# A two-stage kernel on one core: rows of results stored in order, and five pieces of weights put together by TensorE

## The chip, the cores and the metric

The kernel runs on one core of a Trainium2 chip. A core has five engines with a queue of instructions each: TensorE (PE; the loading of its weights, PEld, is listed apart), VectorE (DVE), ScalarE (ACT), GpSimd (POOL) and SyncE (SP), which here issues nearly all transfers. Transfers run on 16 DMA engines. Data lie in HBM, in SBUF (128 partitions) and, for the results of matmuls, in PSUM. The metric is the time of one execution on the device in microseconds (us).

## The reference

Attention without a softmax, with a norm over each head, and then a softplus layer between two matrix products. Cut to what is computed:

```python
# q, k, v: (8, 8, 576, 64), float32; g_norm: (64,)
kv  = np.einsum('bhsd,bhse->bhde', k, v)
o   = np.einsum('bhsd,bhde->bhse', q, kv)
rms = np.sqrt(np.mean(o * o, axis=-1, keepdims=True) + 1e-06)
x   = (o / rms * g_norm)          # -> (4608, 512) after transpose and reshape
# w_in: (512, 2048), w_out: (2048, 512); both arrive as float64
h   = x @ w_in
g   = np.maximum(h, 0.0) + np.log1p(np.exp(-np.abs(h)))
out = (g @ w_out).astype(np.float32)      # (4608, 512)
```

The two large products are made exact enough with float32r matmuls: each operand is split into a high part, a low part scaled by 4096 and a combination of the two, and three matmuls are summed. The weights are 8-byte words, of which the kernel takes the two halves apart and puts float32 numbers together.

## The kernel before

The kernel does not issue instructions directly. It adds tasks to a plan (engine, estimated duration, what it comes after, a priority `pos`, buffers it takes and gives back). `Plan.order` then simulates the engines and gives the order in which every task is issued. So a change of any priority or duration can reorder all five queues. TensorE's idle time before the first big matmul is filled by the plan with matmuls that compute nothing (`warm`).

The sequence of 4608 rows is cut into 36 tiles of 128 rows and 12 blocks of three tiles. The feed-forward part runs in 192 steps: a step takes one block of rows and one of 16 pieces of the inner dimension. The steps are grouped in three phases with partial sums kept in HBM between them.

Constants that the change replaces: the priorities of the first eight pieces of weights (`CONVERT`, and `FETCH` for their loads), of the early tiles, and of the later pieces.

```python
P0 = [-93.0, -6.2, -50.8, -8.7, -11.6, -1.5, -14.9, 2.7, -53.5, -34.8, ...]
CONVERT, FETCH, EARLY, LATER = P0[:8], P0[8:16], P0[16:27], P0[27:]
BY_PE = 12                     # tiles from here on are turned by VectorE
```

One piece of weights (128 x 512) becomes float32 in `weight`. It is cut here to what each instruction does; the line of the profile stands beside it:

```python
a1 = ACT square      # L286: sq <- raw
d1 = DVE high1       # L290: t <- bits of the upper word
d2 = DVE high2       # L294: t <- sign and exponent bits
d3 = DVE mask        # L299: t <- (sq is large enough) * t
     ACT beyond      # L303: sum that shows values out of range
d4 = DVE power       # L307: p <- exponent of t
d5 = DVE rest        # L312: p <- lower word * 2**-52 * p
     DVE total       # L316: w <- t + p
```

Then `divide` splits w in three. For the first four pieces of each matrix (`by_pe`) the last difference is taken by TensorE:

```python
def high():     # ACT, L348
    nc.scalar.activation(dst.tile[:, 0], w.tile, func=AF.Copy, scale=DOWN)
def low():      # DVE, L351: d <- w - high
    nc.vector.tensor_tensor(out=d, in0=w.tile, in1=dst.tile[:, 0], op=ALU.subtract)
def low_up():   # ACT, L355
    nc.scalar.activation(dst.tile[:, 1], d.tile, func=AF.Copy, scale=RADIX)
def less_by_pe():   # PE, L366 and L367
    nc.tensor.matmul(y, lhsT=ident_r, rhs=dst.tile[:, 0], start=True, stop=False)
    nc.tensor.matmul(y, lhsT=minus_r, rhs=dst.tile[:, 1], start=False, stop=True)
def third_of_bank():   # ACT, L370
    nc.scalar.activation(dst.tile[:, 2], bank.tile, func=AF.Copy, scale=-E / (1.0 + E))
```

The attention part of a tile of rows: q is turned (L578 and L585, or by VectorE from the third batch on), multiplied by kv (L523; kv itself is L506), squared (ACT, L591), summed (DVE, L528), its root taken (POOL, L531 and L532), and normed (DVE, L535). The first 12 tiles are turned by TensorE (L540) and stored; of these, the first blocks are also split at once (ACT L437, DVE L440 and L444). Later tiles are turned by VectorE in blocks of 32 x 32 (L615), and the three tiles of a block are put side by side and stored together:

```python
n, i = divmod(t, TB)                      # TB = 3
...   # turn_blocks: xb.tile[:, :, i] <- 32 x 32 blocks of x, turned
def store(a):      # L619
    nc.sync.dma_start(out=xd[n][:, a * TB * BL:(a + 1) * TB * BL].rearrange("(b i) m -> i b m", i=BL),
                      in_=xb.tile[a * BL:(a + 1) * BL].rearrange("i b t j -> i b (t j)"))
...
if i == TB - 1:    # four stores when the third tile is turned
```

So the columns of such a block in HBM are not in the order of the rows of the sequence: groups of 32 rows of the three tiles alternate.

A step, and what ends a block:

```python
def mm1():       # L658, 12 matmuls: h <- x (384 rows) by one piece of w_in
def mm2(i):      # L665, 3 matmuls for each of three tiles: s_i <- g by w_out
# between them: softplus (ACT L678), high (ACT L680), low and less (DVE L669, L673)

def leave(ph, t, bank, done, pos):
    ...          # DVE, L705: ot <- bank * scale + partial sum (loaded by L703)
    if ph == LAST and t >= BY_PE:
        n, i = divmod(t, TB)
        def store():
            m = 0
            while m < P // BL:
                a, u = divmod(P // BL * i + m, TB)
                k = min(TB - u, P // BL - m)
                nc.sync.dma_start(        # L716
                    out=out[n * NT:(n + 1) * NT].rearrange("(t s) f -> t s f", t=TB)[u:u + k, a * BL:(a + 1) * BL],
                    in_=ot.tile[m * BL:(m + k) * BL])
                m += k
        ...
        return
    ...          # all others: nc.sync.dma_start(out=dst, in_=ot.tile), L724, 128 x 512 at once
```

For the blocks whose rows alternate, L716 puts groups of 32 rows back in their places: a tile of results leaves as a piece of 3x32 rows and one of 32, or as two of 2x32 rows.

Of the kernel before, what the change touches and what calls it, by code (L numbers as in the profile page):

```python
# [8 lines left out]
F32 = mybir.dt.float32  # L9
F32R = mybir.dt.float32r  # L10
U32 = mybir.dt.uint32
BF16 = mybir.dt.bfloat16
AF = mybir.ActivationFunctionType
ALU = mybir.AluOpType
# [4 lines left out]
P = 128  # L19
EPS = 1e-6  # L20
RADIX = 4096.0
# [19 lines left out]
class Plan:  # L41
# [13 lines left out]
    def slot(self, ring):  # L55
        return Slot(ring)
# [86 lines left out]
def kernel(  # L143
# [31 lines left out]
    NT = 384  # L175
# [7 lines left out]
    PLACES = 8  # L183
    LAST = PHASES[-1]

    P0 = [-93.0, -6.2, -50.8, -8.7, -11.6, -1.5, -14.9, 2.7, -53.5, -34.8, -51.7, -14.7, -24.2, 1.3,
          -0.2, -4.2, 2.5, -13.0, 8.5, 9.5, 5.5, 23.5, -2.0, 2.5, 2.5, 7.0, 5.0, 14.5, 9.0, 44.5, 49.5,
          68.5, 52.5, 72.0, 95.5, 100.5, 114.5, 111.0, 116.5, 8.5]
    CONVERT, FETCH, EARLY, LATER = P0[:8], P0[8:16], P0[16:27], P0[27:]
    BY_PE = 12  # L190
    AT_ONCE = 2 * TB

# [66 lines left out]
    def weight(j, pos, fetch_pos):  # L259

        c, of_out = divmod(j, 2)
        raw, w = slot("raw"), slot("m")
        words = 2 if wide else 1  # L270

        def fetch():
            src = w_source(j)
            x = new(raw, [P, d_model, words], U32 if wide else F32)
            nc.sync.dma_start(
                out=x.rearrange("p n w -> p (n w)").rearrange("p (a f) -> p a f", a=src.shape[1]), in_=src)

        f = add("SP", 450, fetch, (), fetch_pos, [raw], size=1800, behind=int(pos) - 3)
        if wide:
            sq, t, p = (slot(n) for n in ("sq", "m", "m"))  # L280

            def words_of():
                return raw.tile[:, :, 0], raw.tile[:, :, 1]

            def square():
                nc.scalar.activation(new(sq, [P, d_model], BF16), raw.tile.bitcast(BF16)[:, :, 3],  # L286
                                     func=AF.Square, scale=2.0 ** 47)

            def high1():
                nc.vector.tensor_scalar(out=new(t, [P, d_model], U32), in0=words_of()[1], scalar1=3,  # L290
                                        scalar2=0x3FFFFFF8, op0=ALU.logical_shift_left, op1=ALU.bitwise_and)

            def high2():
                nc.vector.scalar_tensor_tensor(out=t.tile, in0=words_of()[1], scalar=0xC0000000, in1=t.tile,  # L294
                                               op0=ALU.bitwise_and, op1=ALU.bitwise_or)

            def mask():
                tf = t.tile.bitcast(F32)
                nc.vector.scalar_tensor_tensor(out=tf, in0=sq.tile, scalar=2.0 ** 64, in1=tf,  # L299
                                               op0=ALU.is_ge, op1=ALU.mult)  # L300

            def beyond():
                nc.scalar.activation(sq.tile, sq.tile, func=AF.Identity, scale=2.0 ** -126, bias=big,  # L303
                                     accum_out=over[:, j:j + 1])

            def power():
                nc.vector.tensor_scalar(out=new(p, [P, d_model], U32), in0=t.tile, scalar1=0xFF800000,  # L307
                                        scalar2=None, op0=ALU.bitwise_and)

            def rest():  # L310
                pf = p.tile.bitcast(F32)
                nc.vector.scalar_tensor_tensor(out=pf, in0=words_of()[0], scalar=2.0 ** -52, in1=pf,  # L312
                                               op0=ALU.mult, op1=ALU.mult)

            def total():
                nc.vector.tensor_tensor(out=new(w, [P, d_model]), in0=t.tile.bitcast(F32),  # L316
                                        in1=p.tile.bitcast(F32), op=ALU.add)

            a1 = add("ACT", 670, square, [f], pos, [sq], [raw])
            d1 = add("DVE", 430, high1, [f], pos, [t], [raw])  # L320
            d2 = add("DVE", 690, high2, [d1], pos, [], [raw])
            d3 = add("DVE", 690, mask, [d2, a1], pos, [])
            over_done.append(add("ACT", 910, beyond, [d3], pos + (4 if c < 4 else 0), [], [sq]))
            d4 = add("DVE", 430, power, [d3], pos, [p, w])
            d5 = add("DVE", 690, rest, [d4], pos, [], [raw])
            ready = add("DVE", 690, total, [d3, d5], pos, [], [t, p])
        else:
            ready = add("DVE", 450, lambda: nc.vector.tensor_copy(new(w, [P, d_model]), raw.tile[:, :, 0]),
                        [f], pos, [w], [raw])
        if c < PLACES or first_step[c] - last_step[c - PLACES] > 12:  # L330
            divide(j, w, ready, pos, "m", c < 4)
        else:
            spilled = dram.tile([P, d_model], F32, name=f"w_spill{j}")
            st = add("SP", 350, lambda: nc.sync.dma_start(out=spilled, in_=w.tile), [ready], pos, [], [w], 900)
            again = slot("x" if of_out else "m")
            back = max(last_step[c - PLACES] + 0.5, first_step[c] - 3)
            ld = add("SP", 350, lambda: nc.sync.dma_start(out=new(again, [P, d_model]), in_=spilled),
                     [st], back, [again], [], 900, behind=last_step[c - PLACES] - 1)
            divide(j, again, ld, back, "m")

    def divide(j, w, ready, pos, ring, by_pe=False):

# [173 lines left out]
    def rows(t):  # L516
# [88 lines left out]


        n, i = divmod(t, TB)
        if i == 0:
            xb_slots[n] = slot("xb"), []
        xb, turns = xb_slots[n]  # L610

        def turn_blocks():
            if i == 0:
                new(xb, [P, d_model // BL, TB, BL])
            nc.vector.transpose(out=xb.tile[:, :, i], in_=x.tile.rearrange("p h d -> p (h d)").rearrange(  # L615
                "p (b j) -> p b j", j=BL))

        def store(a):
            nc.sync.dma_start(out=xd[n][:, a * TB * BL:(a + 1) * TB * BL].rearrange("(b i) m -> i b m", i=BL),  # L619
                              in_=xb.tile[a * BL:(a + 1) * BL].rearrange("i b t j -> i b (t j)"))  # L620

        turns.append(add("DVE", 710, turn_blocks, [a], pos, [] if i else [xb], [x], follows=turns[-1] if i else None))
        if i == TB - 1:
            stores = [add("SP", 450, lambda a=a: store(a), turns, pos + 0.5, [], [xb], 820) for a in range(P // BL)]
            for u in range(n * TB, t + 1):
                x_there[u] = stores

    def x_of(t):
# [66 lines left out]
    def leave(ph, t, bank, done, pos):  # L695

        ot = slot("m" if ph == 0 else ("m", "x", "m")[t % TB] if ph == LAST else "m")
        if ph == 0:
            a = add("ACT", 600, lambda: nc.scalar.activation(new(ot, [P, d_model]), bank.tile, func=AF.Copy, scale=1.0 + E),
                    [done], pos, [ot], [bank])  # L700
        else:
            pt = slot("m")
            ld = add("SP", 350, lambda: nc.sync.dma_start(out=new(pt, [P, d_model]), in_=part[ph - 1, t][0]),  # L703
                     [part[ph - 1, t][1]], pos - EARLY[10], [pt], [], 900, behind=int(pos) - 4)
            a = add("DVE", 700, lambda: nc.vector.scalar_tensor_tensor(  # L705
                out=new(ot, [P, d_model]), in0=bank.tile, scalar=(scale if ph == LAST else 1.0 + E), in1=pt.tile,
                op0=ALU.mult, op1=ALU.add), [done, ld] + (scale_done if ph == LAST else []), pos, [ot], [bank, pt])
        if ph == LAST and t >= BY_PE:
            n, i = divmod(t, TB)

            def store():
                m = 0
                while m < P // BL:
                    a, u = divmod(P // BL * i + m, TB)
                    k = min(TB - u, P // BL - m)
                    nc.sync.dma_start(  # L716
                        out=out[n * NT:(n + 1) * NT].rearrange("(t s) f -> t s f", t=TB)[u:u + k, a * BL:(a + 1) * BL],
                        in_=ot.tile[m * BL:(m + k) * BL])
                    m += k

            part[ph, t] = None, add("SP", 800, store, [a], pos, [], [ot], 750)
            return
        dst = out[t * P:(t + 1) * P] if ph == LAST else dram.tile([P, d_model], F32, name=f"part{ph}_{t}")
        st = add("SP", 350, lambda: nc.sync.dma_start(out=dst, in_=ot.tile), [a], pos, [], [ot], 720)  # L724
        part[ph, t] = dst, st
# [88 lines left out]
```

## Time and profile before

| | |
|---|---|
| time, median of 3 runs | 934.63 us (933.73 to 934.82) |
| span of the profiled execution | 932.7 us (its time: 934.44 us) |
| mean granted TensorE clock | 0.989 |
| busy PE / PEld / DVE / ACT / POOL | 97% / 88% / 67% / 44% / 9% of the span |
| moved by DMA | 131.43 MB, 141 GB/s in the mean |

The page gives shares of the whole span; the kernel has a head (attention of the first tiles, the first weights), a long middle, and a tail (the last results on their way out). A wait is read in the stretch in which it stands: the timeline shows instructions in order of time, with the idle time before them in brackets; the chain of waits goes back from the last instruction to what released it. In a line of the timeline the first two numbers are start and duration in us. In a line of a group, the number after the bar is the busy time in us, then the mean duration in ns, then the idle time of the engine before them. Matmuls are pipelined, so the distance from one start to the next says more than a duration.

### The profile page before, as it was taken

The page shows a single profiled execution, that of the slowest core. Times are in us where ns is not written, and L with a number is a line of the kernel's source. Part 1 is how long each engine was busy: PE and PEld are TensorE (multiplying, and loading weights), DVE is VectorE, ACT ScalarE, POOL GpSimd, SP SyncE. Part 2 cuts the span into 40 slices and gives each one's busy share as a digit, 9 for nine tenths or more (in the row PEclk, how much of TensorE's full clock was granted, in tenths as well). Part 3 has the DMA queues.
Part 4 walks back from the last instruction along what each step waited for, and adds up shares of the span by engine and source line. Part 5 has one row for each costly group of instructions (what it writes and reads, how often), then busy time and mean ns, then how long its engine had stood idle before and what let it go on. Part 6 is the DMA issues. An engine that isn't in the chain of part 4 may idle for free.

```text
span 932.7 us, 13257 instructions
## 1 busy us (share of the span) xinstructions
PE 904.9 (97%) x4821; PEld 818.5 (88%) x4821; DVE 627.3 (67%) x1055; ACT 414.5 (44%) x799; POOL 80.4 (9%) x78
## 2 busy tenths in 40 slices
PE   7899999999999999999999999999999999999992
PEld 5689899989999999999999999989999998999992
DVE  6777788776458887788757878887434455655531
ACT  4766555444433656464424455555322323333320
POOL 0323421221113100000000000000000000000000
PEclk8999999999999999999999999999999999999997
DMA  8999998498782554346334445551231233444321
GB/s 213 225 225 222 248 212 205 102 212 151 171 143 90 147 147 136 112 145 206 102 102 128 148 157 169 189 182 39 85 102 56 81 102 102 106 119 127 109 75 42
DMA packets 231377, 131.43 MB, mean 141 GB/s; under 512 B 130448, under 2 KB 205200, under 8 KB 231312
## 3 DMA queue, kind: packets, MB, share of 16 engines
q1 hardware_dynamic: 231152, 130.58, 53.3%
q8 instruction: 38, 0.62, 0.3%
q14 instruction: 27, 0.22, 0.1%
q10 hardware_dynamic: 160, 0.00, 0.0%
HBM read 91.75 MB, written 38.80 MB: 140 GB/s over the span
## 4 chain that ended last, share of the span: by engine, by line
PE 93%; SPq 2%; DVE 1%; DMA 1%; POOL 1%; ACT 1%; issue 0%; ACTq 0%
PE s L665 43%; PE h L658 43%; PE o L523 3%; PE o L506 3%; SPq L568 1%; DMA g_col<-in_g_norm_dram 1%; PE tp L540 0%; POOL r L532 0%; DMA m<-in_v_dram 0%; DMA qa<-in_q_dram 0%; DVE m L312 0%; PE tp L578 0%; DVE r L528 0%; DVE xv L440 0%; DVE m L316 0%
## 5 line engine op out<-in xcount | busy, mean ns | idle before, releaser
L658 PE MATMUL h<-xv,w 128*128 128x384 f32 x2304 | 434.6, 337 | 0.0
L665 PE MATMUL s<-w,gv 128*128 128x512 f32 x1728 | 434.3, 395 | 0.0
L658 PEld LDWEIGHTS h<-xv,w 128*128 128x128 f32 x2304 | 406.2, 188 | 14.8 <-issue 0.2
L665 PEld LDWEIGHTS s<-w,gv 128*128 128x128 f32 x1728 | 319.5, 188 | 59.1 <-issue 0.5
L678 ACT ACTIVATE g<-h 128x384 f32<-128x384 f32 x192 | 94.3, 491 | 398.4 <-PE h L658 394.4
L669 DVE TENSOR_TENSOR gv<-g,gv 128x384 fp32r<-128x384 f32 x192 | 106.6, 555 | 175.9 <-ACT gv L680 175.0
L680 ACT ACTIVATE gv<-g 128x384 fp32r<-128x384 f32 x192 | 100.9, 525 | 23.3 <-PE s L665 16.6
L673 DVE SCALAR_TENSOR_TENSOR gv<-gv 128x384 fp32r<-128x384 f32 x192 | 107.0, 557 | 6.0
L440 DVE SCALAR_TENSOR_TENSOR xv<-m,g_col,xv 128x512 fp32r<-128x512 f32 x102 | 75.8, 743 | 1.1 <-ACT xv L437 1.1
L444 DVE SCALAR_TENSOR_TENSOR xv<-xv 128x512 fp32r<-128x512 f32 x108 | 74.5, 690 | 2.6
L437 ACT ACTIVATE xv<-m,g_down 128x512 fp32r<-128x512 f32 x102 | 69.7, 710 | 2.5 <-DMA m<-x 2.4
L532 POOL TENSOR_TENSOR r<-r,half 128x8 f32<-128x8 f32 x36 | 65.8, 1826 | 3.0
L506 PEld LDWEIGHTS o<-m,m 128*128 128x128 f32 x256 | 34.2, 200 | 8.7 <-issue 7.3
L506 PE MATMUL o<-m,m 128*128 128x128 f32 x256 | 35.4, 285 | 6.4 <-DMA m<-in_v_dram 6.4
L705 DVE SCALAR_TENSOR_TENSOR m<-s,scale,m 128x512 f32<-128x512 f32 x24 | 17.9, 747 | 29.7 <-PE s L665 29.7
L523 PE MATMUL o<-kv_diag,m 128*128 128x128 f32 (+1 forms) x296 | 36.9, 275 | 0.0
L523 PEld LDWEIGHTS o<-kv_diag,m 128*128 128x128 f32 (+1 forms) x296 | 35.0, 179 | 1.8 <-issue 1.0
L531 POOL TENSOR_SCALAR r<-r 128x8 f32<-128x8 f32 x36 | 13.9, 386 | 244.9 <-DVE r L528 244.8
L535 DVE TENSOR_TENSOR x<-o,r 128x512 f32<-128x512 f32 x33 | 22.7, 688 | 17.6 <-POOL r L532 17.6
L528 DVE TENSOR_REDUCE r<-x 128x8 f32<-128x512 f32 x36 | 24.5, 681 | 13.3 <-ACT x L591 13.2
L705 DVE SCALAR_TENSOR_TENSOR m<-s,m 128x512 f32<-128x512 f32 x36 | 23.3, 684 | 10.2 <-PE s L665 10.1
L286 ACT ACTIVATE sq<-raw 128x512 bf16<-128x512 bf16 x32 | 21.3, 665 | 16.4 <-DMA raw<-in_moe_w_in_dram 10.2
(67 smaller groups left out, 445.6 us busy)
## 6 DMA issues: line engine op xcount, KB each, us to landing
m<-x SPq DMA_DIRECT2D x102, 256.0 KB
part<-m SPq DMA_DIRECT2D x72, 256.0 KB
m<-part SPq DMA_DIRECT2D x72, 256.0 KB
raw<-in_moe_w_in_dram SPq DMA_DIRECT2D x16, 512.0 KB
m<-in_k_dram SPq DMA_DIRECT2D x64, 128.0 KB
m<-in_v_dram SPq DMA_DIRECT2D x32, 256.0 KB
raw<-in_moe_w_out_dram SPq DMA_DIRECT2D x16, 512.0 KB
qa<-in_q_dram SPq DMA_DIRECT2D x24, 288.0 KB
```

Of the source, the lines that this page charges most:

```text
L437: nc.scalar.activation(cols(0, F32R), x.tile, func=AF.Identity, scale=g_down)
L440: nc.vector.scalar_tensor_tensor(out=cols(1, F32R), in0=x.tile, scalar=g_col, in1=cols(0), op0=ALU.mult, op1=ALU.subtract)
L444: nc.vector.scalar_tensor_tensor(out=cols(2, F32R), in0=cols(1), scalar=-RADIX, in1=cols(0), op0=ALU.mult, op1=ALU.add)
L506: nc.tensor.matmul(kv[:, i if tail else p], lhsT=l, rhs=r, start=(p == 0 and i == 0), stop=tail, skip_group_check=True)
L523: nc.tensor.matmul(y[r0:r0 + n, p::NP], lhsT=qT.tile[:, p, r0:r0 + n], rhs=kv_diag[b % 2][:, p].rearrange("r (h d) -> r h d", d=D), start= ...
L532: nc.gpsimd.tensor_tensor(out=r.tile, in0=r.tile, in1=half, op=ALU.pow)
L658: nc.tensor.matmul(hp, lhsT=w_in.tile[:, i, kd * P:(kd + 1) * P], rhs=xv.tile[:, i, kd], start=(m == 0), stop=(m == 3 * KD - 1))
L665: nc.tensor.matmul(mine[i].tile, lhsT=gv.tile[:, m, i * P:(i + 1) * P], rhs=w_out.tile[:, m], start=(c == cs[0] and m == 0), stop=(c == cs ...
L669: nc.vector.tensor_tensor(out=gv.tile[:, 1], in0=g.tile, in1=gv.tile.bitcast(F32)[:, 0], op=ALU.subtract)
L673: nc.vector.scalar_tensor_tensor(out=gv.tile[:, 2], in0=f32[:, 1], scalar=-RADIX, in1=f32[:, 0], op0=ALU.mult, op1=ALU.add)
L678: a = add("ACT", 490, lambda: nc.scalar.activation(new(g, [P, NT]), h.tile, func=AF.Softplus, scale=1.0 + E), [a], s, [g], [h])
L680: a = add("ACT", 530, lambda: nc.scalar.activation(new(gv, [P, 3, NT], F32R)[:, 0], g.tile, func=AF.Copy, scale=DOWN), [a], s, [gv])
```

## The change

It has three parts.

The results: the last block of rows is turned and stored tile by tile in the order of its rows (`g = 1`), so that its results leave by the plain store of 128 x 512. The results of the other alternating blocks leave in pieces of 32 rows, each a store of its own, where a piece could hold 2x32 or 3x32 rows before. This is meant to spread each store over all DMA engines.

The weights: for the five pieces with the earliest priority, VectorE no longer adds the two halves and no longer takes the low part; TensorE sums both halves less the high part in PSUM with three matmuls, one of them in float32. ScalarE takes the high part of the upper half alone. This is meant to relieve VectorE at the start.

The priorities: all of `P0` may differ, and with it the order of the queues.

```diff
-    P0 = [-93.0, -6.2, -50.8, -8.7, -11.6, -1.5, -14.9, 2.7, -53.5, -34.8, -51.7, -14.7, -24.2, 1.3,
-          -0.2, -4.2, 2.5, -13.0, 8.5, 9.5, 5.5, 23.5, -2.0, 2.5, 2.5, 7.0, 5.0, 14.5, 9.0, 44.5, 49.5,
-          68.5, 52.5, 72.0, 95.5, 100.5, 114.5, 111.0, 116.5, 8.5]
+    P0 = [-98.5, -5.2, -28.3, -7.2, -15.1, -5.0, -33.4, 1.2, -54.5, -41.8, -53.2, -12.2, -29.2, 0.3,
+          -0.7, -5.2, 1.0, -14.5, 9.0, 9.5, 5.5, 24.5, -2.0, 2.5, 2.5, 2.5, -14.5, 14.5, 9.0, 44.5,
+          49.5, 68.5, 52.5, 73.0, 96.0, 100.0, 114.5, 111.0, 116.0, 8.5]
+    BY_TENSOR = sorted(range(8), key=lambda j: CONVERT[j])[:5]
...  # in weight():
+            def rest_rounded():
+                nc.vector.scalar_tensor_tensor(out=new(w, [P, d_model], F32R), in0=words_of()[0], scalar=2.0 ** -52,
+                                               in1=p.tile.bitcast(F32), op0=ALU.mult, op1=ALU.mult)
+            if j in BY_TENSOR:
+                d4 = add("DVE", 430, power, [d3], pos, [p, w])
+                d5 = add("DVE", 690, rest_rounded, [d4], pos, [], [raw, p])
+                divide_by_pe(j, t, w, d3, d5, pos)
+                return
...  # new:
+    def divide_by_pe(j, t, p, t_there, p_there, pos):
+        def high():
+            nc.scalar.activation(new(dst, [P, 3, d_model], F32R)[:, 0], t.tile.bitcast(F32), func=AF.Copy, scale=DOWN)
+        def low():
+            y = new(banks[0], [P, d_model])
+            nc.tensor.matmul(y, lhsT=ident, rhs=t.tile.bitcast(F32), start=True, stop=False)
+            nc.tensor.matmul(y, lhsT=ident_r, rhs=p.tile, start=False, stop=False)
+            nc.tensor.matmul(y, lhsT=minus_r, rhs=dst.tile[:, 0], start=False, stop=True)
+        def low_up():
+            nc.scalar.activation(dst.tile[:, 1], banks[0].tile, func=AF.Copy, scale=RADIX)
...  # less (two matmuls) and third as before, from banks[1]
...  # x of the later tiles:
         n, i = divmod(t, TB)
+        g = TB if n < n_blocks - 1 else 1
+        i0, i = i - i % g, i % g
...
-                new(xb, [P, d_model // BL, TB, BL])
+                new(xb, [P, d_model // BL, g, BL])
...
-            nc.sync.dma_start(out=xd[n][:, a * TB * BL:(a + 1) * TB * BL].rearrange("(b i) m -> i b m", i=BL),
+            nc.sync.dma_start(out=xd[n][:, i0 * P + a * g * BL:i0 * P + (a + 1) * g * BL].rearrange("(b i) m -> i b m", i=BL),
...  # in leave():
-        if ph == LAST and t >= BY_PE:
+        if ph == LAST and BY_PE <= t < n_tiles - TB:
...
-                m = 0
-                while m < P // BL:
+                for m in range(P // BL):
                     a, u = divmod(P // BL * i + m, TB)
-                    k = min(TB - u, P // BL - m)
-                    nc.sync.dma_start(
-                        out=out[n * NT:(n + 1) * NT].rearrange("(t s) f -> t s f", t=TB)[u:u + k, a * BL:(a + 1) * BL],
-                        in_=ot.tile[m * BL:(m + k) * BL])
-                    m += k
+                    row = n * NT + u * P + a * BL
+                    nc.sync.dma_start(out=out[row:row + BL], in_=ot.tile[m * BL:(m + 1) * BL])
```

More of the change, by code (lines that the diff above doesn't have):

```diff
@@ L339, in weight, with less, third @@
             divide(j, again, ld, back, "m")
+    def divide_by_pe(j, t, p, t_there, p_there, pos):
+        c, of_out = divmod(j, 2)
+        dst = slot(f"w{of_out}_{c % PLACES}")
+        w_slots[of_out, c] = dst
+        banks = [slot("h"), slot("h")]
+        def high():
[7 more added lines that the diff above has]
+            nc.scalar.activation(dst.tile[:, 1], banks[0].tile, func=AF.Copy, scale=RADIX)
+        def less():
+            y = new(banks[1], [P, d_model])
+            nc.tensor.matmul(y, lhsT=ident_r, rhs=dst.tile[:, 0], start=True, stop=False)
+            nc.tensor.matmul(y, lhsT=minus_r, rhs=dst.tile[:, 1], start=False, stop=True)
+        def third():
+            nc.scalar.activation(dst.tile[:, 2], banks[1].tile, func=AF.Copy, scale=-E / (1.0 + E))
+        a = add("ACT", 640, high, [t_there], pos, [dst])
+        b = add("PE", 1500, low, [a, p_there], pos, [banks[0]], [t, p])
+        e = add("ACT", 600, low_up, [b], pos, [], [banks[0]])
+        b2 = add("PE", 500, less, [e], pos, [banks[1]])
+        e2 = add("ACT", 600, third, [b2], pos, [], [banks[1]])
+        factors_done[of_out, c] = [a, e, e2]
     def divide(j, w, ready, pos, ring, by_pe=False):
@@ L618, in store @@
         def store(a):
-            nc.sync.dma_start(out=xd[n][:, a * TB * BL:(a + 1) * TB * BL].rearrange("(b i) m -> i b m", i=BL),
+            nc.sync.dma_start(out=xd[n][:, i0 * P + a * g * BL:i0 * P + (a + 1) * g * BL].rearrange("(b i) m -> i b m", i=BL),
                               in_=xb.tile[a * BL:(a + 1) * BL].rearrange("i b t j -> i b (t j)"))
         turns.append(add("DVE", 710, turn_blocks, [a], pos, [] if i else [xb], [x], follows=turns[-1] if i else None))
-        if i == TB - 1:
-            stores = [add("SP", 450, lambda a=a: store(a), turns, pos + 0.5, [], [xb], 820) for a in range(P // BL)]
-            for u in range(n * TB, t + 1):
+        if i == g - 1:
+            stores = [add("SP", 450, lambda a=a: store(a), turns, pos + 0.5, [], [xb], 820 if g > 1 else 490)
+                      for a in range(P // BL)]
+            for u in range(t - i, t + 1):
                 x_there[u] = stores
@@ L707, in leave @@
                 op0=ALU.mult, op1=ALU.add), [done, ld] + (scale_done if ph == LAST else []), pos, [ot], [bank, pt])
-        if ph == LAST and t >= BY_PE:
+        if ph == LAST and BY_PE <= t < n_tiles - TB:
             n, i = divmod(t, TB)
             def store():
-                m = 0
-                while m < P // BL:
+                for m in range(P // BL):
                     a, u = divmod(P // BL * i + m, TB)
-                    k = min(TB - u, P // BL - m)
-                    nc.sync.dma_start(
-                        out=out[n * NT:(n + 1) * NT].rearrange("(t s) f -> t s f", t=TB)[u:u + k, a * BL:(a + 1) * BL],
-                        in_=ot.tile[m * BL:(m + k) * BL])
-                    m += k
-            part[ph, t] = None, add("SP", 800, store, [a], pos, [], [ot], 750)
+                    row = n * NT + u * P + a * BL
+                    nc.sync.dma_start(out=out[row:row + BL], in_=ot.tile[m * BL:(m + 1) * BL])
+            part[ph, t] = None, add("SP", 1600, store, [a], pos, [], [ot], 750)
             return
```

## The prediction

> **What bounds the kernel now.** I read the chain of waits first.
>
> ```profile
> PE 93%; SPq 2%; DVE 1%; DMA 1%; POOL 1%; ACT 1%; issue 0%; ACTq 0%
> ```
>
> TensorE holds 93% of the chain. Its two big groups, and the slices:
>
> ```profile
> L658 PE MATMUL h<-xv,w 128*128 128x384 f32 x2304 | 434.6, 337 | 0.0
> L665 PE MATMUL s<-w,gv 128*128 128x512 f32 x1728 | 434.3, 395 | 0.0
> ...
> PE   7899999999999999999999999999999999999992
> ```
>
> Neither group has idle time before it. In the chain in order of time, twelve L658 take 2.10 us and nine L665 about 2.08 us, so one of the 192 steps costs 4.18 us and all cost 802 us. From 60 us to 916 us the TensorE row has no gap. Only two places can give time: the head, before that unbroken stretch, and the tail after it. The timeline of the tail:
>
> ```profile
> 911.89 4.37 PE L665 MATMUL s<-w,gv 128*128 128x512 f32 x18
> ...
> 916.30 0.75 DVE L705 SCALAR_TENSOR_TENSOR m<-s,scale,m 128x512 f32<-128x512 f32 x1
> ...
> 918.64 1.29 SPq L716 DMA_DIRECT2D out_dram<-m  x2
> ```
>
> The last arithmetic ends at 917.05, the last store is issued by 919.9, the span ends at 932.7: 15.6 us of nothing but stores. The waits of the SyncE queue say what for:
>
> ```profile
> SPq L809 <- DMA out_dram<-m: 11.6, 1, 11.6
> ```
>
> Two stretches show how fast stores go (busy us of PE, PEld, DVE, ACT, POOL, then clock, DMA share, GB/s). At 651 the queue stores whole tiles by L724; at 921 it drains L716's stores:
>
> ```profile
> 651.00:653.00 2.00, 2.00 (x13) 1.91 (x12) 1.32 (x2) 0.35 (x1) 0.00 (x0) 1.00 0.50 183
> 921.00:931.00 10.00, 0.00 (x0) 0.00 (x0) 0.00 (x0) 0.00 (x0) 0.00 (x0) 0.50 0.16 51
> ```
>
> A share of 0.16 is 2.6 engines of 16, and 51 GB/s over them is 20 GB/s each. The drain is not short of bandwidth, it is spread over too few engines.
>
> The head, TensorE first:
>
> ```profile
> 40.20 1.13 PE L506 MATMUL o<-m,m 128*128 128x128 f32 x8 [1.68 <-DMA m<-in_v_dram]
> ...
> 43.35 0.60 PE L540 MATMUL tp<-ident_r,x 128*128 128x128 f32 x4
> ...
> 46.38 2.35 PE L658 MATMUL h<-xv,w 128*128 128x384 f32 x12
> ...
> 54.75 1.13 PE L506 MATMUL o<-m,m 128*128 128x128 f32 x8 [1.34 <-DMA m<-in_v_dram]
> ```
>
> The first step starts at 46.38, after the third tile's turn at 43.35, and that one stands behind a group that waits for v. VectorE meanwhile mixes weights (L316, L351) with rows of x (L535, L440):
>
> ```profile
> 26.20 0.69 DVE L316 TENSOR_TENSOR m<-m,m 128x512 f32<-128x512 f32 x1
> 26.82 0.69 DVE L351 TENSOR_TENSOR m<-m,w 128x512 f32<-128x512 f32 x1
> ...
> 31.32 0.69 DVE L535 TENSOR_TENSOR x<-s,r 128x512 f32<-128x512 f32 x1 [0.76 <-POOL r L532]
> ...
> 40.38 0.68 DVE L535 TENSOR_TENSOR x<-s,r 128x512 f32<-128x512 f32 x1
> ...
> 45.18 0.75 DVE L440 SCALAR_TENSOR_TENSOR xv<-tp,g_col,xv 128x512 fp32r<-128x512 f32 x1 [1.92 <-ACT m L600]
> ```
>
> Start to start, L316 and L351 cost 0.6 us each. VectorE is full from 10.7 to 38 us; after that it waits for the chain through GpSimd, TensorE and ScalarE.
>
> **What the Trainium skill says.** "DMA: Bandwidth & Descriptors", section "Why a DMA increments its semaphore by 16 and not by 1": a copy runs on the largest k up to 16 that divides the slowest dimension above 1 of both patterns, and uses the lowest-numbered engines. L716's pieces of 3x32 rows (from 96 partitions) then get 3 engines, those of 2x32 get 2, and a plain 32-row piece gets 16. The 2.6 engines above agree. The section on the anatomy of one DMA in the same page says that most of the fixed cost is the write receipt; here the span goes on for about 1.2 us after data stop (no GB in the stretch 932 to 933, 6 GB/s in the one before). "FP8 and Floating Point Precision", "TensorE Precision Notes": true fp32 takes four passes. Here four fp32 matmuls of 128 columns (L506) take 0.89 us and one fp32r matmul of 512 columns (L366, L367) 0.23 us: a ratio of nearly four for as many columns.
>
> **Part 1: the stores at the end.** Before, each of the last three tiles is 256 KB. By the rule, engine 0 gets 64 KB of the first tile's 192 KB piece, 64+64 KB of the second tile's two pieces, 64 KB of the third's, and 2x4 KB of the plain pieces: 264 KB, at 20 GB/s 13.5 us. From about 917 that ends near 930.5; the trace has data until 931-932. After, the last block is stored in the order of its rows, so its tiles go by the whole-tile store: 16 KB per engine and tile. The third is ready at 917.05; its issue takes 0.34 us (the duration of L724's), then an estimated 0.6 us to the first byte (L724's at 649.97 had data in the stretch from 650), 16 KB at 20 GB/s take 0.8 us, the receipt 1.2 us: 920.0. If the three tiles instead share the 183 GB/s that L724 showed, 786 KB take 4.3 us from 916.4, and the end is 921.9. I take 921.0: 11.7 us off the tail, all of it on the path. This is the part I trust most.
>
> **Part 2: weights by TensorE.** Each of five pieces loses L316 and L351, 1.2 us of VectorE, 6 us in all, none on ScalarE. TensorE gets three more matmuls a piece: one fp32 of 512 columns (0.89) and two fp32r (0.24 each), 1.4 us, in all 6.8 us. In the order of the changed kernel four of the five come before the first step; there stand 28 warm-up matmuls of L778 where 44 stood, so 16 x 0.24 = 3.8 us of the added 5.5 us take the place of work that does nothing, the rest that of idle time. The order of loads up to q's is the same, and the first x tile waits for them, so 31.3 us for its norm should hold. Then VectorE has less in between: I follow the third tile, its norm at 39.3 instead of 40.4. Its turn still stands behind the group that waits for v at 40.2, but without the group for the tail: near 41.9 instead of 43.35. ScalarE and VectorE follow, and the first step starts near 44.8: 1.6 us earlier, not 6. After it, the fifth piece adds 1.4 us to a full TensorE; the third step now stands ahead of the group that waited 1.34 us at 54.75, which hides that wait; and a piece of weights (512 KB, 2.2 us at the 240 GB/s or so of 50 to 100 us) is now fetched ahead of two of batch 2's keys and values, which may cost 0 to 2 us. Sum: -1.6 + 1.4 - 1.3 + 1.0 = -0.5 us.
>
> **Part 3: the middle.** Blocks 4 to 10 store each tile in four pieces instead of two; four issues of 0.34 us cost the queue what two of 0.7 cost. The last block's x goes out in 12 stores with runs of 128 bytes instead of 4 with 384; the DMA share there is 0.3 to 0.5 and x is read much later. The new constants put loads of partial sums behind the stores of the block before, with 20 us (five steps) to spare. None of it lies on the path: 0.
>
> **Sum.** Span 932.7 - 11.7 - 0.5 = 920.5; the time is 1.8 us above the span now, so 922.3 us, 1.3% less.
>
> **Rivals.** First, VectorE binds the head: it is full from 10.7 to 38 us, and six microseconds less work would bring the first step 5 to 6 us forward, to a time near 917. Against it: the waits for v at 40.2 and for GpSimd stay. Second, TensorE's added work is not hidden: the granted clock is 0.5 in the stretches from 8 to 14 us, the first piece's fp32 matmul falls there and takes twice as long, and kv's groups stand behind it; with loads shifted too, the head loses 3 to 5 us and the time is near 927. Third, stores spread over all engines were hidden anyway and the tail is the receipt of the writes: then nothing changes but the head, and the time stays at 934. The 11.6 us wait with data moving at 51 GB/s speaks against that.
>
> **Range and chances.** The tail is uncertain by 1 us, the head by 3 us either way, and new constants can open a wait in the middle: 919.5 to 927. Faster by over 2% needs 915.9, that is 6 us more from the head: 0.04. Slower by over 2% would take a new stall of 30 us: 0.01. Within 2%: 0.95.
>
> **What would show it.** Right: the SyncE queue's last wait for out_dram falls from 11.6 us to about 2 to 3; the last stretch runs at over 150 GB/s; the span goes on 3 to 5 us after the last VectorE instruction instead of 15.6; the first L658-like group starts at 44 to 46 us; steps stay at 4.18 us. Wrong: gaps in TensorE between 60 us and the end, a first step later than 47 us, or last data still over 10 us after the last arithmetic.

## The result, and the profile after

| | before | after |
|---|---|---|
| time, median | 934.66 us (933.73 to 934.82) | 922.35 us (922.26 to 922.57) |
| span of the profiled execution | 932.7 us | 920.6 us |
| first step starts | 46.38 us | 45.03 us |
| last arithmetic ends | 917.05 us | 917.44 us |
| span goes on after it | 15.6 us | 3.2 us |

The ratio is 0.987, with a 95% interval of 0.985 to 0.989. The chain by engine and the last wait of the SyncE queue, after:

```profile
PE 95%; DMA 2%; SPq 1%; ACT 1%; DVE 1%; issue 0%; ACTq 0%; DVEq 0%
```

```profile
SPq L852 <- DMA out_dram<-m: 1.7, 1, 1.7
```

TensorE's share of the chain is larger because the span lost what was not TensorE: the wait of 11.6 us for the last results is 1.7 us now. The timeline of the tail after, and then two stretches of it (busy us of PE, PEld, DVE, ACT and POOL, clock, DMA share, GB/s):

```profile
912.27 4.38 PE L712 MATMUL s<-w,gv 128*128 128x512 f32 x18
...
916.69 0.75 DVE L752 SCALAR_TENSOR_TENSOR m<-s,scale,m 128x512 f32<-128x512 f32 x1
916.77 0.34 SPq L767 DMA_DIRECT2D out_dram<-x  x1
917.47 0.33 SPq L767 DMA_DIRECT2D out_dram<-m  x1
```

```profile
917.00:919.00 2.00, 0.00 (x0) 0.00 (x0) 0.44 (x1) 0.00 (x0) 0.00 (x0) 1.00 0.99 371
...
919.00:920.00 1.00, 0.00 (x0) 0.00 (x0) 0.00 (x0) 0.00 (x0) 0.00 (x0) 1.00 0.04 12
```

The share is 0.99: all 16 engines move data, at 371 GB/s together and 23 GB/s each. The three tiles (786 KB) are out by 919.1, where 51 GB/s needed until 931 before. The last multiplication and the last addition come no earlier than before. So the whole gain is in the tail, and the head gave nothing. The experiments test both halves of that sentence.

### The profile page after: what moved, and what is told of

Its sections match the earlier page's. It is cut to its first block, busy times and chain, and to the rows that moved or that the text cites. A ratio compares the mean times of both kernels' runs of the same rounds, so it can differ in the third digit from the quotient of the medians.

```text
span 920.6 us, 13308 instructions
## 1 busy us (share of the span) xinstructions
PE 907.2 (99%) x4824; PEld 818.8 (89%) x4824; DVE 620.2 (67%) x1045; ACT 414.6 (45%) x799; POOL 78.7 (9%) x78
## 4 chain that ended last, share of the span: by engine, by line
PE 95%; DMA 2%; SPq 1%; ACT 1%; DVE 1%; issue 0%; ACTq 0%; DVEq 0%
PE s L712 43%; PE h L705 43%; PE o L567 3%; PE o L550 3%; DMA g_col<-in_g_norm_dram 1%; DMA raw<-in_moe_w_in_dram 1%; PE tp L584 1%; SPq L612 0%; DMA qa<-in_q_dram 0%; PE tp L622 0%; PE s L567 0%; SPq L534 0%; PE h L363 0%; ACT sq L304 0%; DVE xv L484 0%
## 5 line engine op out<-in xcount | busy, mean ns | idle before, releaser
L550 PEld LDWEIGHTS o<-m,m 128*128 128x128 f32 x256 | 33.6, 197 | 2.2 <-issue 0.7
L550 PE MATMUL o<-m,m 128*128 128x128 f32 x256 | 34.8, 281 | 0.1
L300 DVE SCALAR_TENSOR_TENSOR m<-sq,m 128x512 f32<-128x512 bf16 x32 | 22.0, 689 | 10.8 <-ACT sq L287 9.5
```

The source lines that it names most:

```text
L550: nc.tensor.matmul(kv[:, i if tail else p], lhsT=l, rhs=r, start=(p == 0 and i == 0), stop=tail, skip_group_check=True)
```

## The experiments

Two theories stood against each other for the tail. Mine: a store is cut over as many DMA engines as the shape of its pieces allows, and the old shapes gave 2 or 3 engines, always the same ones. The rivals: the gain comes from the head, or the old tail was a matter of one queue, or of scattered rows. For the head, mine was that loads and the chain of the first tiles bind it, so that VectorE's saved work and TensorE's added work about cancel; the rival was that VectorE binds it.

### The last block alone

The kernel before, with the last block of rows in order, and nothing else of the change:

```diff
 # kernel before
+        g = TB if n < n_blocks - 1 else 1
+        i0, i = i - i % g, i % g
...
-        if ph == LAST and t >= BY_PE:
+        if ph == LAST and BY_PE <= t < n_tiles - TB:
```

> The kernel before, with only the last block of rows turned and stored in the order of its rows, so that its three tiles of results leave by the whole-tile store; weights, priorities and all other stores are as before. Theory (the gain is the tail alone, because the last stores run on 2 or 3 engines): 922 to 923.5 us, the last data about 2 us after the last arithmetic, the span 3 to 4 us after it. Rival (the head, with weights by TensorE and new priorities, gives a part): above 925 us. Rival (the tail is the receipt of the writes): 934 us.

Measured: 921.36 us, ratio 0.987 (0.985 to 0.988). The last arithmetic ends at 917.69, the span at 920.7, 3.0 us later. One part of the change alone gives the whole of the gain.

### The last block undone

```diff
 # changed kernel
-        g = TB if n < n_blocks - 1 else 1
+        g = TB
...                                     # pieces of 3x32, 2x32 and 32 rows for the last block
-        if ph == LAST and BY_PE <= t < n_tiles - TB:
+        if ph == LAST and t >= BY_PE:
```

> The changed kernel, with only the last block's rows alternating again and its results stored in pieces of 3x32, 2x32 and 32 rows as before. Theory (tail alone): 934 to 935.5 us, as the head of the changed kernel ended no earlier. Rival (the head gives a part): below 932 us.

Measured: 933.62 us, ratio 1.000 (0.999 to 1.001). The last arithmetic ends at 916.49 and the span at 931.8, 15.3 us later. Without its last block the change is worth nothing that can be measured.

### Pieces of 32 rows in place of whole tiles

```diff
 # kernel with the last block undone: for its three tiles too
+                for m in range(P // BL):
+                    a, u = divmod(P // BL * i + m, TB)
+                    row = n * NT + u * P + a * BL
+                    nc.sync.dma_start(out=out[row:row + BL], in_=ot.tile[m * BL:(m + 1) * BL])
```

> The changed kernel, with the last block's rows alternating as before, but each of its tiles stored in four pieces of 32 plain rows: twelve stores at the end in place of three. Theory (what counts is that each store is cut over all 16 engines): the data move at over 150 GB/s, and the end is set by twelve issues of 0.35 to 0.45 us from 915.9 on, so about 921 and then 3 us: 924 to 926 us. Rival (only the whole-tile store in row order is fast, scattered rows are slow): above 930 us.

Measured: 924.48 us, ratio 0.990 (0.989 to 0.992). The SyncE queue at the end of this kernel:

```profile
915.91 1.74 SPq L762 DMA_DIRECT2D out_dram<-m  x4
...
919.63 1.79 SPq L762 DMA_DIRECT2D out_dram<-m  x4
```

and the stretch in which it drains:

```profile
917.00:922.00 5.00, 0.00 (x0) 0.00 (x0) 0.28 (x1) 0.00 (x0) 0.00 (x0) 0.88 0.55 137
```

The rows are as scattered as before, yet they leave at 137 GB/s and not at 51. Scattering is not what was slow. Now the issue binds: each of the twelve stores holds the queue for about 0.45 us (1.79 over 4), the last leaves it at 921.4, and 2.4 us later the span ends.

### A second queue for the old shapes

```diff
 # kernel with the last block undone
-                    nc.sync.dma_start(
+                    (nc.scalar if i == 1 else nc.sync).dma_start(   # last block: the second tile, two pieces of 2x32
```

> The same kernel as with the old tail, but the second of the last three tiles (two pieces of 2x32 rows) is stored from ScalarE's queue, beside the two on SyncE's queue. Theory (a piece of 2x32 or 3x32 rows runs on the lowest-numbered 2 or 3 engines, whatever the queue, and those are what is short): no gain, 934 to 935.5 us. Rival (what is short is the one queue, in which pieces stand behind each other): two queues side by side, 928 to 931 us.

Measured: 933.04 us, ratio 0.999 (0.998 to 1.000), against 933.62 us with one queue. Its timeline and the drain:

```profile
914.90 2.90 SPq L769 DMA_DIRECT2D out_dram<-m  x4
...
915.60 1.74 ACTq L769 DMA_DIRECT2D out_dram<-x  x2
```

```profile
921.00:929.00 8.00, 0.00 (x0) 0.00 (x0) 0.00 (x0) 0.00 (x0) 0.00 (x0) 0.50 0.15 56
```

All issues are over by 917.8 in place of 919.6 with one queue, and still the drain goes on at 56 GB/s with a share of 0.15 (55 and 0.17 in the same stretch with one queue), until past 929. Two queues share the same few engines. That is what the page "DMA: Bandwidth & Descriptors" of the Trainium skill says in the section "Why a DMA increments its semaphore by 16 and not by 1": on the path used here, it is the lowest-numbered k engines. The profile does not name the engines. The share shows how few they are, and this run that both queues use the same ones; that they are the lowest-numbered is the page's word and not shown here.

### The middle stores undone

```diff
 # changed kernel, blocks 4 to 10: pieces of 3x32, 2x32 and 32 rows again
-                for m in range(P // BL):
+                m = 0
+                while m < P // BL:
```

> The changed kernel, with the results of blocks 4 to 10 stored in pieces of 3x32 and 2x32 rows again, the last block as changed. Theory (those stores lie beside a full TensorE): within 0.7 us of the changed kernel on the same chip. Rival (slower stores hold buffers or the queue): over 1 us slower.

Measured: 921.60 us, against 921.41 us for the changed kernel on the same chip. No difference. The slow shapes cost nothing where TensorE is full: TensorE shows no wait from 60 us to its end.

### No weights by TensorE

```diff
 # changed kernel
-    BY_TENSOR = sorted(range(8), key=lambda j: CONVERT[j])[:5]
+    BY_TENSOR = sorted(range(8), key=lambda j: CONVERT[j])[:0]
```

> The changed kernel with its stores and new priorities, but no piece of weights put together by TensorE (VectorE does all five, as before). Theory (what the five pieces cost TensorE and what they save VectorE about cancel): 921.5 to 924 us. Rival (VectorE binds the head, the pieces by TensorE are worth their 6 us): 926 to 929 us. Rival (the added matmuls cost their 1.4 us each): 918 to 920 us.

Measured: 921.15 us, ratio 0.985 (0.983 to 0.987), on another chip, where the kernel before took 935.20 us; the interval overlaps that of the changed kernel. In the trace the first step starts at 46.13, 1.1 us later than with TensorE's help. But from there to the end of the last arithmetic it takes 870.5 us against 872.4. What the pieces bring before the first step they take after it. This fits the theory of cancelling, though the time lies 0.35 us below the range given for it, and the rivals' ranges (918 to 920 and 926 to 929 us) lie further off. Differences of 1 us are not told apart here: one kernel (the table first, below) took 871.7 and 872.8 us for this stretch on two chips.

### The old priorities

```diff
 # changed kernel
-    P0 = [-98.5, -5.2, -28.3, -7.2, -15.1, -5.0, ...]
+    P0 = [-93.0, -6.2, -50.8, -8.7, -11.6, -1.5, ...]
```

> The changed kernel, stores and pieces by TensorE, with the priorities of the kernel before. Theory (the priorities only keep the new tasks from being in the way): 922.5 to 926 us, with the first step later than 45.0 us. Rival (they make no difference): 922 to 922.7 us.

Measured: 921.89 us, ratio 0.985 (0.984 to 0.987), on the chip of the run before; both expected ranges lie above it. The first step starts later, at 46.03, as the theory said, but the time is not longer: from the first step to the last arithmetic it takes 870.8 us. The theory was half wrong: the new priorities move the first step, and no effect on the end can be told.

### Four pieces in place of five

```diff
 # changed kernel
-    BY_TENSOR = sorted(range(8), key=lambda j: CONVERT[j])[:5]
+    BY_TENSOR = [0, 2, 4, 3]
```

> The changed kernel, with the fifth piece, whose matmuls stood after the first step, given back to VectorE; the four before the first step stay with TensorE. Theory (after the first step TensorE is full, so what is taken from it there is time): 1.4 us less than the changed kernel, 920.5 to 921.5 us. Rival (VectorE is just as full there, or the order shifts): 922 us or more.

Measured: 924.04 us (922.98 to 925.21), ratio 0.988 (0.986 to 0.990). The changed kernel has 0.987 (0.985 to 0.989) and did not run on this chip, so that this kernel is slower is not shown; of the 1.4 us that were expected as a gain, nothing is seen. A miss. The plan reordered what follows, and in the profiled run TensorE waits more. From its timeline:

```profile
55.69 1.73 PE L550 MATMUL o<-m,m 128*128 128x128 f32 x8 [1.83 <-DMA m<-in_v_dram]
```

```profile
56.00:58.00 2.00, 2.00 (x12) 2.00 (x11) 0.94 (x2) 0.68 (x1) 0.00 (x0) 0.51 1.21 326
```

From 44.7 to 80 us TensorE is idle for 3.8 us here and for 1.2 us in the changed kernel. And after the wait of 1.83 us the granted clock is recorded at half for about 3 us; the group of eight takes 1.52 us to the next start, at 57.21, in place of 0.89. So the profiled run, the slowest of the four, does not show what a piece taken from TensorE is worth by itself; that stays open. In this run the wait cost more than its length. That is no rule: in the kernel before, waits of 1.68 us at 40.20 and of 1.34 us at 54.75 were followed by a clock of 1.00 and groups of 0.89 us.

### The table first

What does bind the head? SyncE's queue stood still from 9.1 to 12.6 us, because the third load of weights needs a buffer that the first piece still held. That piece waited for ScalarE, which waited 7.0 us for the norm's weights and then loaded two tables (1.28 us each). The chain of waits begins with this transfer of the norm's weights in the kernel before (5.63 us of it) as in the changed one; the prediction followed TensorE and VectorE and did not name it. This run takes the wait away by giving the first use of those weights to GpSimd; one of the two table loads falls away with it:

```diff
 # changed kernel
-    nc.scalar.mul(g_down, g_col, DOWN_G)
     nc.scalar.preload_act_table_set("softplus")
...
+    nc.gpsimd.tensor_scalar(out=g_down, in0=g_col, scalar1=DOWN_G, scalar2=None, op0=ALU.mult)
     nc.vector.memset(half, -0.5)
```

> The changed kernel, with the first scaling of the norm's weights given to GpSimd, so that ScalarE loads its table at once and does not wait 7.0 us for those weights; its first square should start near 5.5 us in place of 10.0. Theory (the head is bound by the loads, and SyncE's queue stood still from 9.1 to 12.6 us for the buffer that the first piece's conversion holds): the loads that follow come about 3 us earlier, first step near 42 us, 919 to 920.5 us. Rival (bandwidth of the DMA engines, busy at 0.85 already, binds the head): within 0.5 us of the changed kernel.

Measured: 919.32 us (918.37 to 922.64), ratio 0.984 (0.982 to 0.986). The spread is wide, so both kernels follow once more on one chip:

> The changed kernel as it is, on the chip of the three that follow, so that they can be compared with it within 1 us: 921.5 to 923 us.

> The table of ScalarE first, once more beside the changed kernel on one chip. Theory (the head is bound by loads that wait for a buffer): 2 to 4 us less than the changed kernel. Rival (the spread of the four earlier runs, 918.4 to 922.6 us, was all): no difference beyond 1 us.

Measured: 921.41 us (921.25 to 922.07) for the changed kernel and 918.61 us (918.00 to 919.33) for this one; the ratios to the kernel before are 0.987 (0.985 to 0.988) and 0.984 (0.982 to 0.985). From these two runs, the start of the chain in the changed kernel, then ScalarE's first square, the load that stood still, q's loads and the first step, in the changed kernel and with the table first:

```profile
1.30 6.15 DMA g_col<-in_g_norm_dram
```

```profile
10.55 0.64 ACT L287 ACTIVATE sq<-raw 128x512 bf16<-128x512 bf16 x1
...
13.19 0.35 SPq L276 DMA_DIRECT2D raw<-in_moe_w_out_dram  x1
...
18.16 4.49 SPq L612 DMA_DIRECT2D qa<-in_q_dram  x6
...
44.58 2.35 PE L705 MATMUL h<-xv,w 128*128 128x384 f32 x12
```

```profile
5.50 0.68 ACT L287 ACTIVATE sq<-raw 128x512 bf16<-128x512 bf16 x1 [1.95 <-DMA raw<-in_moe_w_in_dram]
...
9.51 0.38 SPq L276 DMA_DIRECT2D raw<-in_moe_w_out_dram  x1
...
14.52 5.57 SPq L612 DMA_DIRECT2D qa<-in_q_dram  x6
...
41.64 2.35 PE L705 MATMUL h<-xv,w 128*128 128x384 f32 x12
```

The square comes 5.1 us earlier, the load that stood still 3.7 us, q's loads 3.6 us, the first step 2.9 us, the time 2.8 us. So ScalarE's wait for the norm's weights bound the head, and the rival of bandwidth falls: the engines moved 239 GB/s in the first 20 us in place of 201. That the wait acts by way of the loads is only in part shown. The run also brings ScalarE's and VectorE's own work on the first piece forward, and after the first square the chain goes on by SyncE's loads in the first profile of the changed kernel, but by the matmuls of the first pieces in the second.

### The table first, and no weights by TensorE

```diff
 # kernel with the table first
-    BY_TENSOR = sorted(range(8), key=lambda j: CONVERT[j])[:5]
+    BY_TENSOR = sorted(range(8), key=lambda j: CONVERT[j])[:0]
```

> The table of ScalarE first, and no piece of weights put together by TensorE. Theory (with loads earlier the head is still bound by loads and the chain, and the pieces by TensorE cost as much as they save): within 1 us of the run with the table first. Rival (with the loads out of the way VectorE binds the head): 2 to 5 us slower than that run.

Measured: 918.12 us (917.65 to 920.68), ratio 0.984 (0.982 to 0.985), on the chip of the last two. The first step starts at 42.14, 0.5 us later than with TensorE's help, and from there it takes 871.3 us against 872.8. The runs of the two kernels overlap (918.00 to 919.33 us with the pieces by TensorE), so with the loads earlier, too, nothing is seen of what these pieces are worth. Both kernels were faster than the changed one in all of their runs beside it.

## Why the prediction was right, and where it was not

**What bounds the kernel.** Right. The long middle has the same steps, and the groups of TensorE have the same busy time within 0.2 us. Only head and tail differ.

**Part 1, the tail.** Right in mechanism and nearly in size. The prediction gave 11.7 us; the span after the last arithmetic shrank by 15.6 - 3.2 = 12.4 us. Mis-sized was the rate of the three tiles together: 183 GB/s were taken from the stretch at 651 us, and 371 were measured. The stretch at 651 has a DMA share of 0.50, which is 8 engines of 16 at 23 GB/s each, so it was no limit; 16 engines at that rate give what was measured. The other estimate, 920.0, was nearer. What the prediction calls the receipt, the time from the last data to the end of the span, was put at 1.2 us and was about 1.4 (919.2 to 920.6); no run shows what passes in it.

The count of engines fits more closely than the prediction said. By its sum the first two engines have 264 KB each and the third 136 KB, so only two should still be at work in the last microseconds before. The share there is 0.13, or 2.1 engines of 16:

```profile
926.00:930.00 4.00, 0.00 (x0) 0.00 (x0) 0.00 (x0) 0.00 (x0) 0.00 (x0) 0.50 0.13 51
```

With the last block alone (3.0 us after the last arithmetic) and with it undone (15.3 us), this part is shown.

**Part 2, the head.** This is the step that failed: the weights by TensorE and the new order were to bring 0.5 us, and the last arithmetic came 0.4 us later (917.44 against 917.05; 917.15 in the second profile of the changed kernel). What the first step won, the stretch after it lost. The terms:
- The first step "near 44.8" came at 45.03, but not by the way predicted. The first tile's norm was to hold at 31.3 and came at 32.15: VectorE waited 3.04 us for a square that stood in ScalarE's queue behind a step that waited for TensorE's new matmuls. The third tile's norm was to come at 39.3 and came at 41.14. Its turn started at 41.97, right after that norm, where the prediction had it wait for v. The time of the first step came out right for a wrong reason, which is luck. VectorE on the first and third tile, then TensorE, after:

```profile
20.57 0.69 DVE L300 SCALAR_TENSOR_TENSOR m<-sq,m 128x512 f32<-128x512 bf16 x1 [3.04 <-ACT sq L287]
...
32.15 0.69 DVE L579 TENSOR_TENSOR x<-s,r 128x512 f32<-128x512 f32 x1
...
41.14 0.68 DVE L579 TENSOR_TENSOR x<-s,r 128x512 f32<-128x512 f32 x1
...
41.97 0.63 PE L584 MATMUL tp<-ident_r,x 128*128 128x128 f32 x4
...
45.03 2.35 PE L705 MATMUL h<-xv,w 128*128 128x384 f32 x12
```

- One piece's three matmuls were to take 1.4 us; in the chain they take 0.86 + 0.24 + 0.23 = 1.33. Right. For the fifth piece they stand after the first step, from 60.47 on.
- The wait of 1.34 us at 54.75 was to vanish, and did: the group stands at 54.20 without one. The weights fetched earlier were to cost 1.0 us; what came are waits of 0.81 us at 58.17 and 0.32 us at 62.27 for ScalarE and VectorE. TensorE's idle time after the first step went from 1.34 to 1.2 us, so these two terms gave -0.1 and not -0.3. About 0.5 us of the 1.7 us by which the stretch after the first step grew is not explained by these terms. It is less than the 1.1 us by which two profiles of one kernel differ in this stretch, so it need not have a cause in the change. With the old priorities the stretch takes 870.8 us: TensorE's idle time in it is 0.2 us, and the same two large groups of matmuls are busy 0.7 us less.

**Part 3, the middle.** Right: 0, shown by the run with the old shapes in blocks 4 to 10. The issue of a piece of 32 rows was put at 0.34 us and takes 0.42 in the median; it is off the path.

**The sum.** The time was predicted as 922.3 and measured as 922.35 us. That is closer than its terms, and luck: the tail was better by 0.7 us and the head worse by 0.9.

**The rivals.** "VectorE binds the head" would have made 917 us; the runs without weights by TensorE, with loads early and late, show that VectorE's work is not what the end waits for. From 10.7 to 38 us, which the prediction called full, VectorE was busy for 24.0 us before and for 18.7 us after, and yet the first tile's norm came later. "The added work is not hidden" was partly right: the first piece's three matmuls do fall into slow TensorE time (2.05 us for its float32 pair in place of 1.02) and ScalarE waits for such matmuls, but the first tile came only 0.85 us later. "The stores were hidden anyway" is refuted by the last block alone.

## What to carry to other kernels

Count, for the last stores of a kernel, over how many DMA engines each is cut; a shape that costs nothing in the middle can cost 12 us at the end, where nothing lies beside it. When work is moved from a busy engine to the one that bounds the kernel, ask what the busy engine's time was worth at that place: here 6 us less on VectorE and 7 us more on TensorE came out at zero within about 1 us. And follow the chain of waits to its very start: a transfer for which ScalarE waited 7 us held up the head, and taking that wait away was worth 2.8 us at the end. Before a rate is carried over, look at the share beside it: 183 GB/s at a share of 0.50 were no limit.

## What was not expected

In these runs a store's issue differs with its shape: 0.34 us for 128x512, 0.42 us for 32x512, 0.59 us for a piece of 2x32 rows (medians), and 0.71 to 0.74 us for pieces of 3x32 rows.

The record of the granted clock is not always whole. After, it says 1.00 for all of the head, but between 14.21 and 15.78 us a group of eight L550 takes 1.57 us where it takes 0.89 us later. In the second profile of the same kernel the clock is recorded at 0.50 from 10 to 15 us. So the mean clock of 1.000 after against 0.989 before is no gain: before, it counts the slow head and over 12 us of the drain at 0.50, in which TensorE did nothing.
